# Phi and the memory's term of a pair of heads moved within its slots, and two low parts moved from GpSimd to VectorE

## The chip, the cores and the metric

The kernel runs on one core of a Trainium2 chip. The core has five engines, each with a queue of its own that it works off in order: TensorE (PE, matrix products), VectorE (DVE), ScalarE (ACT), GpSimd (POOL) and SyncE (SP), which here issues every DMA. The metric is the time of one execution on the device in microseconds (us), taken as the median of several runs.

## The reference, cut to what matters

```python
scores = scale * np.matmul(q, k.transpose(0, 1, 3, 2))     # B=2, H=8, S=576, D=64
scores = np.where(causal, -1000000000.0, scores)
a = np.exp(scores - scores.max(-1, keepdims=True)); a /= a.sum(-1, keepdims=True) + 1e-09
local = np.matmul(a, v)
phi = lambda x: np.where(x > 0, x, np.exp(x) - 1.0) + 1.0
q_p = phi(q)
mem_out = (q_p @ M_prev) / (q_p @ z_prev + 1e-06)          # the memory's term
x = sigmoid(beta) * mem_out + (1 - sigmoid(beta)) * local   # -> (1152, 512)
y = ((x @ w1) * (x @ w2)) @ w3 @ w_out                      # 512 -> 1024 -> 1024 -> 512
out = sum over 4 experts of p_e * (relu(y @ e_w1[e]) @ e_w2[e])
```

## The kernel before

**Precision.** Most products are made of two parts of each operand: a high part in a rounded format (a copy or cast) and a low part, which is the difference of the number and its high part. Each product is three passes (`PASSES`): high by low, low by high, high by high. So each operand costs one cast and one subtraction; `lo_pool` makes the subtraction on GpSimd (line 79), `lo_dve` on VectorE (line 82).

**Attention.** The 16 heads are worked on as 8 pairs; pair p has head 2p on partitions 0 to 63 and head 2p + 1 on partitions 64 to 127. `load_pair` loads q and k of a pair (tiles `qd`, `kd`, two buffers each), `stage_h` makes their high and low parts (`qs`, `ks`, one buffer each), `stage_a` the scores (`sc`, line 214) with mask, minimum (DVE, line 220) and exponential (ACT, line 227), `stage_b` the transposes of the probabilities (`pt`, line 254, copied to `pT` by ACT), their product with v (`a`, line 267), the memory's term (`mem`: `b`, line 291, scaled on DVE by `rm` into `xm`), the joining (`join`: `ra` and `xq` on DVE, then `xq + xm` on GpSimd, line 299) and the transposes of the result (`fin`: `x`, line 310, then `xT`). `stage_phi` makes phi of q: an exponential on ACT (`ex`, line 182), a minimum and a maximum with a sum on DVE (lines 185 and 186).

**Slots.** `run_slot(n, ...)` writes the steps of several pairs into one list, each with a number between 0 and 1, and emits them in the order of these numbers: the high and low parts of pair n + 2, phi and scores of pair n + 1, and `stage_b` of pair n, with the fill steps of the weight branch spread between them. `MEM_AT` is the number of the memory's term, `PHI_AT` those of phi. A scheduler then orders the instructions of each engine by its own model of their durations; the order of the program is its priority, not its result.

**The weight branch.** In slots -1 to 0 the eight row tiles of `w_out` are loaded, brought from 64-bit to fp32 by `from64` (two ACT and two DVE instructions, lines 101 to 105, the tile `tu` having one buffer and `tf` three) and split (`wo`). In slots 0 to 3 the product of w3 and w_out is made, one accumulation after another (`wacc0`, `wacc1`, ... line 377; 24 products of 128x512 each, 12 from each of two tiles `w3s`). A `w3s` tile is made by `from64` and then by GpSimd (high part line 76, low part line 79); there are two buffers of it. There is one PSUM buffer for `wacc`, so the first product of `wacc1` waits until ACT and DVE have taken the high and low parts of `wacc0` out (`W0`, lines 382 and 383). In slots 4 to 7 the products with w1 and w2 (`ab`, line 442) and with W (`c`, line 505) take the place of `wacc`; then the second batch's, then the experts (`d` line 613, `o` line 630).

**PSUM for attention.** Scores, `a`, `b` and `x` share two buffers (tag "S").

Of the kernel before, what the change touches and what calls it, by code (L numbers as in the profile page):

```python
# [16 lines left out]


H_AT = (0.5, 0.6, 0.52, 0.62)
PHI_AT = (0.6, 0.7)  # L20
A_AT = (0.2, 0.27, 0.34, 0.41)
T_AT = (0.01, 0.05, 0.09, 0.13, 0.17, 0.21, 0.25, 0.29)
MEM_AT, PV_AT, JOIN_AT, FIN_AT = 0.11, (0.4, 0.48), 0.54, 0.68

WO_SLOTS = (-0.9, -0.8, -0.7, -0.6, -0.3, -0.1, 0.1, 0.2)
W_SLOTS, B_SLOTS, C_SLOTS = (0.0, 4.0), (4.0, 6.4), (6.4, 8.0)
# [7 lines left out]
def kernel(  # L34
# [18 lines left out]
    B, H, D, S = qT.shape  # L53
# [18 lines left out]
    def r32(ap):  # L72
        return ap.bitcast(F32)
# [4 lines left out]
    def lo_pool(dst, src, hi):  # L78
        nc.gpsimd.tensor_sub(dst, src, r32(hi))  # L79

    def lo_dve(dst, src, hi):
        nc.vector.tensor_sub(dst, src, r32(hi))  # L82
# [46 lines left out]
    raw_t, qk_t, phi_t, prob_t = {}, {}, {}, {}  # L129
# [24 lines left out]
    def stage_h(p):  # L154

        if p >= B * H // 2:
            return []
        qd, kd = raw_t[p]
        qk_t[p] = [A1.tile([P, 2, S], F32R, tag=f"{x}s", name=f"{x}s{p}") for x in "qk"]
        qs, ks = qk_t[p]  # L160
        return [
            *zip(
                H_AT,
                (
                    lambda: nc.scalar.copy(qs[:, 0, :], qd),
                    lambda: nc.scalar.copy(ks[:, 0, :], kd),
                    lambda: lo_pool(qs[:, 1, :], qd, qs[:, 0, :]),
                    lambda: lo_pool(ks[:, 1, :], kd, ks[:, 0, :]),
                ),
            )  # L170
        ]

    def stage_phi(p):

        if p >= B * H // 2:
            return []
        qd = raw_t.pop(p)[0]
        ex = A1.tile([P, S], F32, tag="ex", name=f"ex{p}")
        phi_t[p] = phi = A2.tile([P, S], F32, tag="phi", name=f"phi{p}")

        def f0():
            nc.scalar.activation(ex, qd, AF.Exp)

        def f1():
            nc.vector.tensor_scalar(out=ex, in0=ex, scalar1=1.0, scalar2=None, op0=ALU.min)  # L185
            nc.vector.scalar_tensor_tensor(out=phi, in0=qd, scalar=0.0, in1=ex, op0=ALU.max, op1=ALU.add)

        return [*zip(PHI_AT, (f0, f1))]

# [48 lines left out]
    def stage_b(p):  # L238


        b, h = divmod(2 * p, H)
        phi = phi_t[p]
        pt, st = {}, {}
        xq = A2.tile([RP, NQ, 2, D], F32, tag="xq", name=f"xq{p}")

        def trans(x, g):
            def f():
                Pt = prob_t[2 * p + x]
                mine = blocks[g * NB : (g + 1) * NB]
                ps = psT.tile([P, 512], F32, tag="T", name=f"pt{g}_{2 * p + x}")[0:RP, 0 : RP * len(mine)]  # L250
                t = A2.tile([RP, RP * len(mine)], F32, tag=f"pt{g}", name=f"pT{g}_{2 * p + x}")
                for y, (i, j) in enumerate(mine):
                    sl = slice(y * RP, (y + 1) * RP)
                    nc.tensor.transpose(ps[:, sl], Pt[i][:, q0[j] : q0[j] + RP], identF[0:RP, 0:RP])  # L254
                    pt[x, i, j] = t[:, sl]
                nc.scalar.copy(t, ps)
            return f

        def pv(x):
            def f():  # L260
                vn = v4[(2 * p + x) % 4]
                if x == 0:
                    ps = psS.tile([P, 2, 512], F32, tag="S", name=f"a{p}")[0:RP, :, 0 : NQ * (D + 1)]
                    st["a"] = ps.rearrange("p x (i d) -> p x i d", d=D + 1)
                for i in range(NQ):
                    for j in range(i + 1):
                        nc.tensor.matmul(  # L267
                            st["a"][:, x, i, :], lhsT=pt[x, i, j][0 : rows[j]], rhs=vn[0 : rows[j], j, :],
                            start=(j == 0), stop=(j == i),
                        )  # L270
            return f

        def scaled(dst, ps, eps, gate, nm):

            r = A2.tile([RP, 2, NQ], F32, tag=f"r{nm}", name=f"r{nm}{p}")
            for x in range(2):
                nc.vector.tensor_scalar(
                    out=r[:, x, :], in0=ps[:, x, :, D], scalar1=eps, scalar2=gate[0:RP, h + x : h + x + 1],
                    op0=ALU.add, op1=ALU.mult,
                )  # L280
            nc.vector.reciprocal(r, r)
            for x in range(2):
                nc.vector.tensor_mul(dst(x), ps[:, x, :, 0:D], r[:, x, :].unsqueeze(2).to_broadcast([RP, NQ, D]))

        def mem():
            ps = psS.tile([P, 2, 512], F32, tag="S", name=f"b{p}")[0:RP, :, 0 : NQ * (D + 1)]
            m = ps.rearrange("p x (i d) -> p x i d", d=D + 1)
            for i in range(NQ):
                for x in range(2):
                    o = slice(x * D, (x + 1) * D)  # L290
                    nc.tensor.matmul(  # L291
                        m[:, x, i, :], lhsT=phi[o, q0[i] : q0[i] + RP], rhs=mz[o, p, :], start=True, stop=True
                    )
            st["m"] = A2.tile([RP, NQ, 2, D], F32, tag="xm", name=f"xm{p}", bufs=1)
            scaled(lambda x: st["m"][:, :, x, :], m, 1e-6, gm, "m")

        def join():
            scaled(lambda x: xq[:, :, x, :], st["a"], 1e-9, gl, "a")
            nc.gpsimd.tensor_add(xq, xq, st["m"])

        def fin():
            if b:
                xT[b, h // 2] = main.tile([P, 2, S], F32R, tag=f"g{p}", name=f"xT{b}_{h // 2}")
            xt = xT[b, h // 2]

            o0 = 512 - q0[NQ - 1]
            ps = psS.tile([P, 1024], F32, tag="S", name=f"x{p}")[:, o0 : o0 + S]
            for c in range(NQ):
                w = rows[c]
                nc.tensor.transpose(  # L310
                    ps[:, q0[c] : q0[c] + w], xq[0:w, c].rearrange("p h d -> p (h d)"), identF[0:w, 0:w]
                )
            nc.scalar.copy(xt[:, 0, :], ps)
            lo_dve(xt[:, 1, :], ps, xt[:, 0, :])

        return [
            *zip(T_AT, (trans(x, g) for x in range(2) for g in range(4))),
            (MEM_AT, mem), (PV_AT[0], pv(0)), (PV_AT[1], pv(1)), (JOIN_AT, join), (FIN_AT, fin),
        ]

    def run_slot(n, fill):
        steps = stage_h(n + 2) + stage_phi(n + 1) + stage_a(n + 1)
        steps += stage_b(n) if n >= 0 else []
        steps += [((i + 0.5) / len(fill), f) for i, f in enumerate(fill)]
        for _, f in sorted(steps, key=lambda t: t[0]):
            f()
# [152 lines left out]
    for _, f in stage_h(0):  # L479
        f()  # L480
# [57 lines left out]
    for n in range(-1, B * H // 2):  # L538
        if n + 2 < B * H // 2:
            load_pair(n + 2)  # L540
        if n + 1 < B * H // 2:
            load_head(2 * n + 2), load_head(2 * n + 3)
        run_slot(n, sum([f for at, f in fills if n <= at < n + 1], []))
# [59 lines left out]
    for e in range(E):  # L603
        nxt = None
        for c, (c0, cw) in enumerate(CHUNKS):
            hs = []
            for m in range(KF):
                ps = ps3.tile([P, 512], F32, tag="P", name=f"d{e}_{c}_{m}")[:, 0:cw]
                n = 0
# [15 lines left out]
            for tt in range(cw // P):  # L625
                po = ps3.tile([P, 512], F32, tag="P", name=f"o{e}_{c}_{tt}")
                n = 0
# [59 lines left out]
```

## Time and profile before

| | us |
|---|---|
| median of 3 runs | 762.63 (762.61 to 763.99) |
| the profiled execution | 763.01 |
| its span, first to last instruction | 761.2 |
| TensorE busy | 742.5 (98%) |
| VectorE busy | 283.9 (37%) |
| ScalarE busy | 234.7 (31%) |
| GpSimd busy | 224.9 (30%) |

The profiled execution has 1.8 us around its span. TensorE carries the kernel: the chain that ended last lies 95% on it. What it does not spend busy lies nearly all at the start (the first 60 us) and at the end, after the last product.

### The profile page before, as it was taken

The numbers are of one execution on the slowest core, as the hardware profiler recorded it, in microseconds if no ns is written. First come the engines' busy times: TensorE is split into PE (matmuls) and PEld (weight loads), VectorE is DVE, ScalarE is ACT, GpSimd is POOL, SyncE is SP. The second block draws the span as 40 slices with busy tenths as digits, with TensorE's granted clock in tenths as the row PEclk, the third lists the DMA queues.
The fourth block names the chain that finished last, engine by engine and source line by source line (L and its number), as shares of the span: only waits on it lengthen the run. The fifth ranks groups of instructions, "written<-read, shape, count | busy, mean of one in ns | idle before, by whom it ended". The sixth has DMA issues, their size and how long they took to land.

```text
span 761.2 us, 11248 instructions
## 1 busy us (share of the span) xinstructions
PE 742.5 (98%) x4568; PEld 656.5 (86%) x4568; DVE 283.9 (37%) x626; ACT 234.7 (31%) x471; POOL 224.9 (30%) x228
## 2 busy tenths in 40 slices
PE   3899999999999999999999999999999999999997
PEld 2778888899999999999889888898988999888986
DVE  6977557567644135333212112121221112111221
ACT  7976557565644323322202011010111011010110
POOL 2164543444540036004920087000590004300000
PEclk9999999999999999999999999999999999999999
DMA  9873313444510014201410033000241001101010
GB/s 268 282 217 115 104 48 122 134 141 126 174 52 28 2 56 152 58 27 44 126 55 0 1 97 125 0 1 1 57 126 39 1 1 42 28 1 56 0 42 28
DMA packets 48755, 56.69 MB, mean 74 GB/s; under 512 B 15808, under 2 KB 32192, under 8 KB 48704
## 3 DMA queue, kind: packets, MB, share of 16 engines
q1 hardware_dynamic: 48704, 55.97, 24.4%
q8 instruction: 36, 0.59, 0.3%
q14 instruction: 15, 0.12, 0.1%
HBM read 49.41 MB, written 6.55 MB: 74 GB/s over the span
## 4 chain that ended last, share of the span: by engine, by line
PE 95%; DVE 2%; ACT 1%; issue 1%; DMA 0%; SPq 0%; DVEq 0%; ACTq 0%
PE d L613 26%; PE o L630 26%; PE ab L442 14%; PE a L267 7%; PE c L505 7%; PE wacc L377 6%; PE sc L214 4%; PE pt L254 4%; PE b L291 1%; PE x L310 1%; DMA qd<-in_qT_dram 0%; DVE tf_wo L104 0%; DVE tf_wo L105 0%; DVE wo L82 0%; DVE ex L185 0%
## 5 line engine op out<-in xcount | busy, mean ns | idle before, releaser
L630 PE MATMUL o<-el,he 128*128 128x512 f32 x864 | 201.3, 393 | 0.0
L630 PEld LDWEIGHTS o<-el,he 128*128 128x128 f32 x864 | 161.8, 188 | 36.6
L619 ACT ACTIVATE he<-d 128x512 fp32r<-128x512 f32 (+2 forms) x96 | 47.2, 491 | 342.4 <-PE d L613 342.4
L76 POOL TENSOR_SCALAR el<-rel 128x512 fp32r<-128x512 f32 x64 | 40.1, 632 | 258.6 <-PE d L613 188.3
L613 PE MATMUL d<-x2b,el 128*128 128x384 f32 (+1 forms) x768 | 113.7, 308 | 0.0
L613 PEld LDWEIGHTS d<-x2b,el 128*128 128x128 f32 x768 | 113.1, 189 | 0.7
L442 PE MATMUL ab<-xT,ws 128*128 128x288 f32 x768 | 113.1, 298 | 0.0
L620 DVE SCALAR_TENSOR_TENSOR he<-d,he 128x512 fp32r<-128x512 f32 (+2 forms) x96 | 53.5, 558 | 147.7 <-ACT he L619 147.7
L442 PEld LDWEIGHTS ab<-xT,ws 128*128 128x128 f32 x768 | 104.0, 188 | 1.8 <-issue 0.4
L613 PE MATMUL d<-x2a,el 128*128 128x512 f32 x384 | 89.6, 394 | 0.0
L613 PEld LDWEIGHTS d<-x2a,el 128*128 128x128 f32 x384 | 72.0, 188 | 16.8
L79 POOL TENSOR_TENSOR el<-rel,el 128x512 fp32r<-128x512 f32 x64 | 83.4, 1317 | 1.8
L639 DVE SCALAR_TENSOR_TENSOR acc<-o,pr,acc 128x512 f32<-128x512 f32 x27 | 20.3, 751 | 125.7 <-PE o L630 125.7
L505 PE MATMUL c<-hT,W 128*128 128x288 f32 x384 | 58.2, 298 | 0.3 <-DVE x2b L82 0.3
L267 PEld LDWEIGHTS a<-v,pT 114*120 114x120 f32 (+1 forms) x480 | 55.1, 193 | 2.6 <-issue 1.9
L267 PE MATMUL a<-v,pT 114*120 114x65 f32 (+1 forms) x480 | 56.2, 276 | 0.0
L505 PEld LDWEIGHTS c<-hT,W 128*128 128x128 f32 x384 | 52.6, 188 | 0.9 <-DVE x2b L82 0.5
L377 PE MATMUL wacc<-wo,w3s 128*128 128x512 f32 x192 | 50.7, 413 | 0.0
L214 PE MATMUL sc<-ks,qs 64*120 64x120 f32 (+5 forms) x288 | 38.1, 377 | 12.0 <-POOL ks L79 9.4
L227 ACT ACTIVATE P<-P,mn 120x120 f32<-120x120 f32 (+3 forms) x80 | 42.6, 581 | 6.1 <-DVE mn L220 5.9
L377 PEld LDWEIGHTS wacc<-wo,w3s 128*128 128x128 f32 x192 | 36.4, 196 | 8.1 <-issue 0.9
L214 PEld LDWEIGHTS sc<-ks,qs 64*120 64x120 f32 x288 | 25.1, 211 | 21.0 <-POOL ks L79 9.8
(76 smaller groups left out, 598.0 us busy)
## 6 DMA issues: line engine op xcount, KB each, us to landing
rel<-in_moe_w_dram SPq DMA_DIRECT2D x64, 256.0 KB, 2.7
wr<-in_moe_w_dram SPq DMA_DIRECT2D x16, 512.0 KB, 4.1
w3r<-in_moe_w3T_dram SPq DMA_DIRECT2D x16, 512.0 KB, 4.0
wor<-in_moe_w_out_dram SPq DMA_DIRECT2D x8, 512.0 KB, 7.2
wf<-tf SPq DMA_DIRECT2D x16, 256.0 KB, 2.2
wr<-wf SPq DMA_DIRECT2D x16, 256.0 KB, 3.1
v<-in_v_dram SPq DMA_DIRECT2D x16, 150.0 KB, 3.8
qd<-in_qT_dram SPq DMA_DIRECT2D x8, 288.0 KB, 3.5
```

Of the source, the lines that this page charges most:

```text
L76: nc.gpsimd.tensor_scalar(out=dst, in0=src, scalar1=1.0, scalar2=1.0, op0=ALU.mult, op1=ALU.mult)
L79: nc.gpsimd.tensor_sub(dst, src, r32(hi))
L214: nc.tensor.matmul(ps[x][:, c : c + k1 - k0], lhsT=qs[o, a, q0[i] : q0[i] + RP], rhs=ks[o, b, k0:k1], start=(m == 0), stop=(m == 2),)
L227: nc.scalar.activation(Pt[i], Pt[i], AF.Exp, bias=mn[:, i : i + 1], scale=-1.0)
L267: nc.tensor.matmul(st["a"][:, x, i, :], lhsT=pt[x, i, j][0 : rows[j]], rhs=vn[0 : rows[j], j, :], start=(j == 0), stop=(j == i),)
L377: nc.tensor.matmul(wacc[t], lhsT=w3s[u][:, a, c, :], rhs=wo[4 * g + c][:, bb, :], start=(g == 0 and c == 0 and x == 0), stop=(g == 1 and c ...
L442: nc.tensor.matmul(ps[:, 0:HS], lhsT=self.ws[u][:, wi, kk, :], rhs=xT[b, kk][:, xi, a * HS : (a + 1) * HS], start=(n == 0), stop=(n == 3 * ...
L505: nc.tensor.matmul(st["ps"][:, 0:HS], lhsT=Wt[kk][:, wi, d * P : (d + 1) * P], rhs=hT[kk][:, xi, a * HS : (a + 1) * HS], start=(kk == 0 an ...
L613: nc.tensor.matmul(ps, lhsT=ew1[m // 4 * 4 + kk][:, wi, m % 4 * P : (m % 4 + 1) * P], rhs=rhs[:, xi, :], start=(n == 0), stop=(n == 3 * KD ...
L619: nc.scalar.activation(ht[:, 0, :], ps, AF.Relu)
L620: nc.vector.scalar_tensor_tensor(out=ht[:, 1, :], in0=ps, scalar=0.0, in1=r32(ht[:, 0, :]), op0=ALU.max, op1=ALU.subtract,)
L630: nc.tensor.matmul(po, lhsT=hs[kk][:, xi, tt * P : (tt + 1) * P], rhs=ew2[kk][:, wi, :], start=(n == 0), stop=(n == 3 * KF - 1),)
```

## The change

Three things are altered.

1. phi of pair n is made in slot n (numbers 0.22 and 0.3) and not in slot n - 1 (0.6 and 0.7).
2. The memory's term of pair n has the number 0.45 in place of 0.11, which is behind all scores of pair n + 1 in the same slot.
3. The low parts of q and k of the first pair are made on VectorE in place of GpSimd.

```diff
-PHI_AT = (0.6, 0.7)
+PHI_AT = (0.22, 0.3)
-MEM_AT, PV_AT, JOIN_AT, FIN_AT = 0.11, (0.4, 0.48), 0.54, 0.68
+MEM_AT, PV_AT, JOIN_AT, FIN_AT = 0.45, (0.4, 0.48), 0.54, 0.68
...
         qs, ks = qk_t[p]
+        lo = lo_pool if p else lo_dve
...
-                    lambda: lo_pool(qs[:, 1, :], qd, qs[:, 0, :]),
-                    lambda: lo_pool(ks[:, 1, :], kd, ks[:, 0, :]),
+                    lambda: lo(qs[:, 1, :], qd, qs[:, 0, :]),
+                    lambda: lo(ks[:, 1, :], kd, ks[:, 0, :]),
...
     def stage_phi(p):
-        if p >= B * H // 2:
-            return []
...
-        phi = phi_t[p]
+        phi = phi_t.pop(p)
...
-        steps = stage_h(n + 2) + stage_phi(n + 1) + stage_a(n + 1)
-        steps += stage_b(n) if n >= 0 else []
+        steps = stage_h(n + 2) + stage_a(n + 1)
+        steps += stage_phi(n) + stage_b(n) if n >= 0 else []
```

The scheduler makes a new order of the whole attention part from it. In the rows below a name's first number is its place in the program (`w3s2` is the third w3 tile, `qs2` belongs to the third pair, `W0` to the first accumulation) and the number behind the underscore that of its buffer. Three places of slot 0 are shown, each before and after.

GpSimd, from the first w3 tile on, before:

```order
L76 TENSOR_SCALAR w3s0_371<-tf_l30_365 128x512
L79 TENSOR_TENSOR w3s0_371<-tf_l30_365,w3s0_371 128x512
L76 TENSOR_SCALAR w3s1_380<-tf_l31_374 128x512
L79 TENSOR_TENSOR w3s1_380<-tf_l31_374,w3s1_380 128x512
L76 TENSOR_SCALAR w3s2_489<-tf_l32_483 128x512
L79 TENSOR_TENSOR w3s2_489<-tf_l32_483,w3s2_489 128x512
L79 TENSOR_TENSOR qs2_305<-qd2_299,qs2_305 128x576
L79 TENSOR_TENSOR ks2_306<-kd2_301,ks2_306 128x576
```

And after:

```order
L76 TENSOR_SCALAR w3s0_366<-tf_l30_360 128x512
L79 TENSOR_TENSOR w3s0_366<-tf_l30_360,w3s0_366 128x512
L76 TENSOR_SCALAR w3s1_375<-tf_l31_369 128x512
L79 TENSOR_TENSOR w3s1_375<-tf_l31_369,w3s1_375 128x512
L79 TENSOR_TENSOR qs2_300<-qd2_294,qs2_300 128x576
L79 TENSOR_TENSOR ks2_301<-kd2_296,ks2_301 128x576
L76 TENSOR_SCALAR w3s2_467<-tf_l32_461 128x512
L79 TENSOR_TENSOR w3s2_467<-tf_l32_461,w3s2_467 128x512
```

The two low parts of the third pair stand ahead of the third w3 tile now, and stood behind it.

VectorE, from the sixth w3 tile's conversion to the low part of `W0`, before:

```order
L104 SCALAR_TENSOR_TENSOR tf_l35_638<-tf_l35_638,tu_l35_639 128x512
L105 SCALAR_TENSOR_TENSOR tf_l35_638<-w3r5_585,tf_l35_638 128x512
L277 TENSOR_SCALAR ra0_578<-a0_514,gl_59 120x5 x2
L281 RECIPROCAL ra0_578<-ra0_578 120x10
L283 TENSOR_TENSOR xq0_321<-a0_514,ra0_578 120x5x64 x2
L82 TENSOR_TENSOR W0_60<-wacc0_409,W0_60 128x512
```

And after:

```order
L104 SCALAR_TENSOR_TENSOR tf_l35_633<-tf_l35_633,tu_l35_634 128x512
L105 SCALAR_TENSOR_TENSOR tf_l35_633<-w3r5_583,tf_l35_633 128x512
L276 TENSOR_SCALAR rm0_539<-b0_527,gm_58 120x5 x2
L185 SCALAR_TENSOR_TENSOR phi2_971<-qd2_294,ex2_970 128x576
L280 RECIPROCAL rm0_539<-rm0_539 120x10
L282 TENSOR_TENSOR xm0_538<-b0_527,rm0_539 120x5x64 x2
L184 TENSOR_SCALAR ex3_1278<-ex3_1278 128x576
L276 TENSOR_SCALAR ra0_576<-a0_494,gl_59 120x5 x2
L280 RECIPROCAL ra0_576<-ra0_576 120x10
L282 TENSOR_TENSOR xq0_316<-a0_494,ra0_576 120x5x64 x2
L82 TENSOR_TENSOR W0_60<-wacc0_386,W0_60 128x512
```

Five steps stand ahead of `ra` and `W0` that were elsewhere: the scaling of the first pair's memory term, the second half of phi of pair 2 and the first half of that of pair 3.

TensorE, from the last products of `wacc0` to the first of `wacc1`, before:

```order
L377 MATMUL wacc0_409<-wo7_121,w3s1_380 128x512 x3
L254 MATMUL pt0_2_670<-identF_81,P0_2_309 120x120
L254 MATMUL pt0_2_670<-identF_81,P1_2_310 120x120 x2
L254 MATMUL pt0_2_670<-identF_81,P2_2_311 120x120
L254 MATMUL pt1_2_679<-identF_81,P2_2_311 120x120 x2
L254 MATMUL pt1_2_679<-identF_81,P3_2_312 120x120 x2
L254 MATMUL pt2_2_690<-identF_81,P3_2_312 120x120 x2
L254 MATMUL pt2_2_690<-identF_81,P4_2_313 120x120 x2
L254 MATMUL pt3_2_718<-identF_81,P4_2_313 120x120 x3
L377 MATMUL wacc1_587<-wo0_114,w3s2_489 128x512 x3
```

And after, from the memory's term of the first pair on:

```order
L290 MATMUL b0_527<-mz_99,phi0_315 120x65 x10
L266 MATMUL a0_494<-v1_101,pT0_1_391 120x65 x3
L266 MATMUL a0_494<-v1_101,pT1_1_422 120x65 x4
L266 MATMUL a0_494<-v1_101,pT2_1_433 120x65 x4
L266 MATMUL a0_494<-v1_101,pT3_1_471 120x65 x3
L376 MATMUL wacc0_386<-wo7_121,w3s1_375 128x512 x3
L253 MATMUL pt0_2_665<-identF_81,P0_2_302 120x120
L253 MATMUL pt0_2_665<-identF_81,P1_2_303 120x120 x2
L253 MATMUL pt0_2_665<-identF_81,P2_2_304 120x120
L253 MATMUL pt1_2_674<-identF_81,P2_2_304 120x120 x2
L253 MATMUL pt1_2_674<-identF_81,P3_2_305 120x120 x2
L376 MATMUL wacc1_585<-wo0_114,w3s2_467 128x512 x3
```

Fifteen transposes stood between the two accumulations, and eight do now; the memory's term of the first pair, which stood among the transposes before the second pair's scores, is now inside the second half of `a`.

## Rows read from the trace of the kernel before

**Rows 1.** Page, part 1: busy us (share of span) and instructions of TensorE.

```profile
PE 742.5 (98%) x4568; PEld 656.5 (86%) x4568; DVE 283.9 (37%) x626; ACT 234.7 (31%) x471; POOL 224.9 (30%) x228
```

**Rows 2.** Busy us by stretch: PE, PEld, DVE, ACT, POOL; then granted clock, DMA share, GB/s.

```profile
0.00:20.00 20.00, 8.40 (x48) 5.92 (x50) 14.01 (x37) 14.51 (x27) 4.58 (x14) 1.00 0.94 266
...
60.00:80.00 20.00, 20.00 (x165) 16.83 (x164) 15.89 (x42) 15.15 (x28) 8.33 (x9) 1.00 0.44 132
```

**Rows 3.** Timeline of the start: start us, us, engine, line, operation [idle before].

```profile
4.86 0.67 ACT L165 CAST qs<-qd 128x576 fp32r<-128x576 f32 x1 [0.68 <-DMA qd<-in_qT_dram]
5.62 1.40 POOL L79 TENSOR_TENSOR qs<-qd,qs 128x576 fp32r<-128x576 f32 x1 [3.45 <-DMA kd<-in_kT_dram]
...
6.02 0.66 ACT L166 CAST ks<-kd 128x576 fp32r<-128x576 f32 x1
...
6.97 1.62 POOL L79 TENSOR_TENSOR ks<-kd,ks 128x576 fp32r<-128x576 f32 x1
7.37 1.84 DVE L186 SCALAR_TENSOR_TENSOR phi<-qd,ex 128x576 f32<-128x576 f32 x1
...
8.64 2.88 PE L214 MATMUL sc<-ks,qs 64*120 64x120 f32 x24 [8.64 <-POOL ks L79]
```

**Rows 4.** Timeline of VectorE: phi's two steps and a low part, GpSimd idle.

```profile
14.68 0.45 DVE L185 TENSOR_SCALAR ex<-ex 128x576 f32<-128x576 f32 x1
...
16.82 0.76 DVE L186 SCALAR_TENSOR_TENSOR phi<-qd,ex 128x576 f32<-128x576 f32 x1
...
64.00 0.75 DVE L82 TENSOR_TENSOR xT<-x,xT 128x576 fp32r<-128x576 f32 x1
```

**Rows 5.** Timeline: the memory's term of two pairs, and ScalarE's wait for a load.

```profile
19.35 1.87 PE L291 MATMUL b<-mz,phi 64*120 64x65 f32 x16
...
26.43 0.68 ACT L101 ACTIVATE tu_wo<-wor 128x512 uint32<-128x512 uint16 x1 [0.23 <-DMA wor<-in_moe_w_out_dram]
...
87.09 1.27 PE L291 MATMUL b<-mz,phi 64*120 64x65 f32 x20
```

**Rows 6.** Timeline of TensorE from the end of wacc0 to wacc1.

```profile
52.54 0.96 PE L377 MATMUL wacc<-wo,w3s 128*128 128x512 f32 x3
53.35 0.98 PE L254 MATMUL pt<-identF,P 120*120 120x120 f32 x8
54.65 0.99 PE L254 MATMUL pt<-identF,P 120*120 120x120 f32 x7 [0.32 <-ACT pT L256]
55.41 5.72 PE L377 MATMUL wacc<-wo,w3s 128*128 128x512 f32 x24
```

**Rows 7.** Timeline of GpSimd: the third w3 tile, then the third pair's q.

```profile
47.02 0.81 POOL L76 TENSOR_SCALAR w3s<-tf_l 128x512 fp32r<-128x512 f32 x1 [2.49 <-PE wacc L377]
47.91 1.30 POOL L79 TENSOR_TENSOR w3s<-tf_l,w3s 128x512 fp32r<-128x512 f32 x1
49.17 1.42 POOL L79 TENSOR_TENSOR qs<-qd,qs 128x576 fp32r<-128x576 f32 x1
```

**Rows 8.** Timeline of ScalarE at that place.

```profile
47.62 0.68 ACT L165 CAST qs<-qd 128x576 fp32r<-128x576 f32 x1 [0.30 <-PE sc L214]
...
50.12 0.67 ACT L102 ACTIVATE tf_l<-w3r 128x512 f32<-128x512 f32 x1
```

**Rows 9.** Timeline of VectorE up to the low part of W0.

```profile
50.83 1.68 DVE L104 SCALAR_TENSOR_TENSOR tf_l<-tf_l,tu_l 128x512 uint32<-128x512 uint32 x1 [1.77 <-ACT tf_l L102]
52.54 0.69 DVE L105 SCALAR_TENSOR_TENSOR tf_l<-w3r,tf_l 128x512 uint32<-128x512 uint32 x1
53.15 0.35 DVE L277 TENSOR_SCALAR ra<-a,gl 120x5 f32<-120x5 f32 x2
...
54.59 0.68 DVE L82 TENSOR_TENSOR W<-wacc,W 128x512 fp32r<-128x512 f32 x1
```

**Rows 10.** Timeline of TensorE: the first products of wacc0.

```profile
42.32 4.84 PE L377 MATMUL wacc<-wo,w3s 128*128 128x512 f32 x12
```

**Rows 11.** A stretch of these products, columns as in rows 2.

```profile
44.00:46.00 2.00, 2.00 (x6) 1.52 (x6) 1.85 (x3) 1.26 (x2) 0.54 (x1) 1.00 0.69 194
```

## The prediction

> **What bounds the kernel now.** I read the shares of the engines first, then busy time by stretch, then the waits, and last the timelines of single engines in the first 60 us. TensorE is busy for 742.5 of 761.2 us [rows 1]. The stretches show where the rest lies: of the first 20 us TensorE has 8.4 busy, and from 60 us on a stretch of 20 us is full [rows 2]. So from there no wait of another engine counts, and the change can act only on what TensorE does in the first 60 us, or by making a wait where there is none. The first product starts at 8.64, released by the low part of the first pair's k on GpSimd [rows 3]. The next thing to see is the step from the first w3 accumulation to the second: 3 products from 52.54, 15 transposes, and `wacc1` from 55.41 on [rows 6]. There is one buffer for these sums, and the low part of `W0` that frees it starts on VectorE at 54.59 and lasts 0.68, so it ends at 55.27 [rows 9]. The 15 transposes cover this with 0.14 us to spare. That is the tightest place after the start, and the order shows that the change takes its cover away.
>
> **The start (third part of the change).** GpSimd takes 1.40 and 1.62 for the two low parts [rows 3]; VectorE takes 0.75 for one of that size [rows 4]. On VectorE the first can start when the cast of q ends (5.53), the minimum of `ex` (0.45) stands between, and the second needs the cast of k (6.68) [rows 3, 4]. It ends at about 7.5 in place of 8.59: TensorE starts 1.1 us earlier. VectorE pays two times 0.75 and gets back that phi no longer runs beside GpSimd, 1.84 against 0.76 [rows 3, 4]. This gain does not reach the end. At 26.43 ScalarE waits for a slice of `w_out` [rows 5]; the queue of loads has the same order up to there, so that slice lands when it did, and with the new order the exponentials of the second pair and two copies of transposes are queued behind that instruction. I follow the copies: TensorE needs the third `pT` of the first head copied before it can go on with the second head's transposes, and eight instructions of ScalarE stand between that and the one that waited at 26.43. Followed on from there by the durations of the same instructions before, I get both kernels level at about 42 us, with the first pair's memory term still to do in the changed one. Bounds: 0 to 1.1 us gained; I take 0.
>
> **The memory's term (second part).** In the kernel before it ran in TensorE's idle time: 16 of its products from 19.35, at a point where the second pair's q and k were not ready [rows 5]. Now the first pair's stands inside the second half of `a`, where TensorE is full. That costs 20 products, 1.27 us [rows 5]. The wait below swallows it, since TensorE has to wait there anyway; it counts only if that wait is absent. In the later slots the term is moved from one full place to another, and the number of stretches of one kind on TensorE stays about the same (274 before, 269 now): 0, with a bound of 0.5 us to either side.
>
> **Phi (first part).** The scheduler hoists phi: phi's minimum of the first three pairs still stands among the first 40 instructions of VectorE. What the new numbers change is where the rest lands, and that is ahead of `W0`. The load of a q tile now waits for phi's second step; behind it on SyncE's queue stand loads of k, v and w3 tiles. q is loaded a slot or more before its scores, so I take 0 for this.
>
> **The new wait at wacc1.** Here the sum is made. (a) GpSimd made the third w3 tile at 47.02 and 47.91 and then q's low part from 49.17 [rows 7]; the order is now q, k, third tile. The cast of the third pair's q starts at 47.62 and lasts 0.68 [rows 8]. I take it there again: it stands at the end of the same series of conversions of w3 tiles, whose links between ScalarE, VectorE and GpSimd are unchanged. So q's low part runs from 48.3 to 49.7, k's to 51.1 (1.42 each), the tile's high part to 51.9 (0.81), its low part to 53.2 (1.30). Before, it ended at 49.2. (b) ScalarE's next `tf` needs that tile's buffer. It started at 50.12 [rows 8], it now starts at 53.2, +3.1, and ends at 53.9. (c) VectorE waits for it: line 104 took 1.68 beside GpSimd's k, and has no GpSimd beside it now, so I take the 0.69 of line 105 for both [rows 9]: the pair ends at 55.3 in place of 53.2. (d) Ahead of `ra` there are now `rm`, its reciprocal and `xm`, which are the twins of `ra`, its reciprocal and `xq` (53.15 to 54.59, 1.44 us [rows 9]), a phi step of 0.76 and a minimum of 0.45 [rows 4]: 2.65 us. `ra` starts at 57.9, the low part of `W0` at 59.4 and ends at 60.1. (e) `wacc1` starts at 60.2 and not at 55.41, 4.8 us later, and seven transposes (55.41 less 54.65, 0.76 us [rows 6]) are still owed. That is 5.5 us. (f) Two things make it less: the cast of q waited 0.30 for TensorE [rows 8], which has done those scores earlier now, and instructions of VectorE follow each other about 0.08 closer than they last (52.54 to 53.15 is 0.61 for a duration of 0.69 [rows 9]), over about six steps 0.5. **Sum: +4.7 us.** TensorE comes to that place at about 55 and waits for about 4 us; behind it in its queue is everything. Bounds: +3.2 if the 1.1 us of the start and GpSimd's shorter times get through, +6 if VectorE's steps run into GpSimd's next high part.
>
> Against the profiled execution (763.01, of which 1.8 lies around the span) this gives 767.7. The median of the runs shown is 762.63, 0.4 below; from it 767.3. I forecast 767.5. A measurement of this kernel can tell about 0.2% (1.5 us) from no change.
>
> **The rivals.** *The gap costs the clock.* Of the first products of `wacc0`, 12 take 4.84 us [rows 10], while the 24 of `wacc1` take 5.72 [rows 6]: 0.40 against 0.24 each, which are the two levels of 1.2 and 2.4 GHz, although the granted clock is shown as 1.00 in that stretch too [rows 11]. TensorE had only scores, transposes and short products before, and the durations fell behind these twelve. If the 4 us of idle time at `wacc1` set the clock back, the next twelve products last 4.84 instead of 2.9, and the time is 2 us more: 769.5. For it: the gap would be the longest since the start. Against it: no gap after the rise is in the trace. The Trainium skill (TensorE: Matmul & The Clock Gate, Part 1: The HAM clock gate) says that idle time throttles the clock and sustained work releases it; by that rule the time would be this 769.5, and no row here shows a fall.
>
> *No wait at wacc1.* The place is the same, the point is when the third w3 tile's low part ends on GpSimd. If it ends by 50 in place of 53, because ScalarE's series of conversions runs three us ahead (its wait at 26.43 gone, the early scores passed on), `W0` is out at about 56.5 and TensorE hardly waits. Then the memory's term is paid, 1.27, less the wait of 0.32 in the transposes [rows 5, 6]: 763.6, no change that can be told. Against it: ScalarE's and VectorE's series also needs TensorE to release the first w3 tile, which was at 47.02 [rows 7].
>
> *The start gets through.* As the second, and the 1.1 us of the start as well as another microsecond of the 11.6 that TensorE is idle in the first 20 [rows 2] are kept: about 761. It needs both, and the load that ScalarE waits for speaks against it [rows 5].
>
> *Phi is not moved at all* (the scheduler hoists it): this is nearly so, and alone would change nothing; the memory's term and the places above are moved all the same.
>
> **How the numbers follow.** Forecast 0.53 (765.5 to 768.5, slower). Clock set back 0.20 (769.5, slower). No wait or a wait under a microsecond 0.19 (763.6; nearly all within 0.2%, 0.03 of it slower). Faster 0.08. So slower 0.76, same 0.16, faster 0.08. The range for 8 in 10 runs from 763.4, which takes in most of the case without a wait, to 770.0, above the case of the clock.
>
> **What would show it.** In the changed kernel's trace: the first scores at about 7.5; `b` of the first pair behind the first 20 products of `wacc0`; an idle gap of 3 to 5 us on TensorE ahead of `wacc1`, put down to VectorE's line 82 (the low part of `W0`); GpSimd with the third w3 tile's low part ending at about 53; no waits of TensorE above a microsecond after 62 us. The durations of the products behind the gap (0.24 or 0.40) decide on the clock. The forecast is wrong if `W0` is out before the eight transposes are done, or if TensorE waits in later slots too, for `xq` or for the w3 tile that GpSimd makes behind the joining.

## The result

| | us |
|---|---|
| before, median of 8 runs beside it | 762.76 (762.42 to 765.95) |
| changed, median of 8 runs | 767.25 (766.90 to 768.24) |
| ratio changed / before | 1.0057, 95% interval 1.0048 to 1.0066 |
| span of the profiled execution, before / changed | 761.2 / 765.2 |

The changed kernel is 4.5 us slower. The forecast was 767.5 with a chance of 0.76 for slower; size and sign came out, but not by the sum that I wrote: three of its terms were off, and the errors nearly cancel.

### The profile after

First the page's line of engine shares for the changed kernel, which answers to [rows 1], and busy time by stretch, columns as in [rows 2]:

```profile
PE 740.3 (97%) x4568; PEld 655.6 (86%) x4568; DVE 288.7 (38%) x628; ACT 235.4 (31%) x471; POOL 223.1 (29%) x226
```

```profile
0.00:20.00 20.00, 8.62 (x46) 5.96 (x46) 14.11 (x40) 15.89 (x30) 1.60 (x12) 1.00 0.92 271
60.00:80.00 20.00, 20.00 (x134) 16.23 (x133) 10.32 (x30) 12.43 (x24) 6.13 (x7) 0.94 0.33 105
```

TensorE is busy for 2.2 us less than before and the span is 4.0 us longer, so it waits 6.2 us more. And from 60 to 80 us, where the first kernel's granted clock was 1.00, it is 0.94.

The waits of TensorE, longest first (who waits, for whom: us in total, times, longest):

```profile
PE sc L213 <- DVE ks L82: 7.6, 1, 7.6
PE wacc L376 <- DVE W L82: 4.1, 1, 4.1
PE sc L213 <- POOL ks L79: 3.0, 1, 3.0
PE pt L253 <- ACT P L226: 2.4, 2, 1.8
```

The first is the start, 1.0 us shorter than the 8.64 of [rows 3]. The second is the new wait at `wacc1`. The third is the stretch that the first pair's memory term has left. TensorE's timeline at the place of [rows 6]:

```profile
52.21 0.95 PE L376 MATMUL wacc<-wo,w3s 128*128 128x512 f32 x3
53.00 0.98 PE L253 MATMUL pt<-identF,P 120*120 120x120 f32 x8
58.07 4.81 PE L376 MATMUL wacc<-wo,w3s 128*128 128x512 f32 x13 [4.09 <-DVE W L82]
```

And the three engines ahead of it, GpSimd [rows 7], ScalarE [rows 8] and VectorE [rows 9], in this order:

```profile
46.47 1.45 POOL L79 TENSOR_TENSOR qs<-qd,qs 128x576 fp32r<-128x576 f32 x1 [3.46 <-ACT qs L166]
47.86 1.42 POOL L79 TENSOR_TENSOR ks<-kd,ks 128x576 fp32r<-128x576 f32 x1
49.23 0.63 POOL L76 TENSOR_SCALAR w3s<-tf_l 128x512 fp32r<-128x512 f32 x1
49.94 1.27 POOL L79 TENSOR_TENSOR w3s<-tf_l,w3s 128x512 fp32r<-128x512 f32 x1
```

```profile
45.72 0.67 ACT L166 CAST qs<-qd 128x576 fp32r<-128x576 f32 x1
...
51.24 0.67 ACT L102 ACTIVATE tf_l<-w3r 128x512 f32<-128x512 f32 x1 [2.93 <-POOL w3s L79]
```

```profile
51.95 0.69 DVE L104 SCALAR_TENSOR_TENSOR tf_l<-tf_l,tu_l 128x512 uint32<-128x512 uint32 x1 [4.76 <-ACT tf_l L102]
...
55.80 0.35 DVE L276 TENSOR_SCALAR ra<-a,gl 120x5 f32<-120x5 f32 x2
...
57.24 0.68 DVE L82 TENSOR_TENSOR W<-wacc,W 128x512 fp32r<-128x512 f32 x1
```

This is the chain of the prediction, link by link: q and k on GpSimd, the third w3 tile behind them, ScalarE's `tf` that waits for the tile, VectorE that waits for `tf` (idle for 4.76 us with `W0` queued behind), and TensorE that waits for `W0`. Only the times are earlier than I had them: the cast of q starts at 45.72, not at 47.62, and `W0` at 57.24, not at 59.4.

TensorE's own windows behind the gap (busy, then granted clock, DMA share, GB/s):

```profile
56.00:58.00 2.00, 0.00 (x0) 1.00 0.89 268
58.00:60.00 2.00, 1.93 (x6) 0.71 0.14 29
60.00:62.00 2.00, 2.00 (x6) 0.50 0.00 0
62.00:64.00 2.00, 2.00 (x16) 0.94 0.15 38
```

The clock was granted in full up to the gap and falls to 0.50, the level of 1.2 GHz, just behind it. The 13 products take 4.64 us from the first to the next instruction (58.07 to 62.71), against 13 x 0.232 = 3.0 at full clock (the 24 of [rows 6] took 5.57 to the next instruction): 1.6 us. The rule of the Trainium skill that the prediction cited for this rival (TensorE: Matmul & The Clock Gate, Part 1: The HAM clock gate) is that idle time throttles the clock; this trace agrees, with 0.50 behind 4.09 us without a product. No fall followed the gap of 3.21 us in the run with the memory's term alone, further down.

**The sum as the trace has it.** `wacc1` starts 2.66 us later (58.07 for 55.41) and owes seven transposes (0.76): 3.4. The clock takes 1.6. That is 5.0 at the end of the second accumulation. At the first product of the experts (`d`) it is 4.0 (360.17 against 356.18). So 1.0 us is regained on the way, with TensorE waiting 0.8 us there for new reasons (`x` for `xq` 0.4, `ab` for ScalarE 0.4).

The gain is in the memory's later terms. One of them in the kernel before, in TensorE's timeline, and one in the changed kernel:

```profile
213.99 0.43 PE L291 MATMUL b<-mz,phi 64*120 64x65 f32 x4
214.34 1.85 PE L442 MATMUL ab<-xT,ws 128*128 128x288 f32 x12
216.12 0.64 PE L291 MATMUL b<-mz,phi 64*120 64x65 f32 x8
216.69 1.87 PE L442 MATMUL ab<-xT,ws 128*128 128x288 f32 x12
218.48 0.63 PE L291 MATMUL b<-mz,phi 64*120 64x65 f32 x6
```

```profile
170.46 1.27 PE L290 MATMUL b<-mz,phi 64*120 64x65 f32 x20
171.66 2.00 PE L441 MATMUL ab<-xT,ws 128*128 128x288 f32 x13
```

Before, three of the later terms are split into pieces between the products `ab`, and each piece holds TensorE longer than its share: 4 products 0.35, 8 products 0.57, while 20 in a row hold it 1.20. Start to start, the terms of 141, 175 and 214 us took 1.83, 1.35 and 1.83 us; behind the scores they stand in one row, and 1.4 us are saved over the three.

### The profile page after: what moved, and what is told of

Its sections match the earlier page's. It is cut to its first block, busy times and chain, and to the rows that moved or that the text cites. A ratio compares the mean times of both kernels' runs of the same rounds, so it can differ in the third digit from the quotient of the medians.

```text
span 765.2 us, 11257 instructions
## 1 busy us (share of the span) xinstructions
PE 740.3 (97%) x4568; PEld 655.6 (86%) x4568; DVE 288.7 (38%) x628; ACT 235.4 (31%) x471; POOL 223.1 (29%) x226
## 4 chain that ended last, share of the span: by engine, by line
PE 90%; DVE 3%; ACT 2%; issue 1%; POOL 1%; DMA 1%; SPq 0%; POOLq 0%; DVEq 0%; ACTq 0%
PE d L612 26%; PE o L629 26%; PE ab L441 13%; PE c L504 7%; PE a L266 6%; PE wacc L376 5%; PE sc L213 3%; PE pt L253 3%; PE b L290 1%; DMA wor<-in_moe_w_out_dram 1%; POOL w3s L79 1%; PE x L309 1%; DVE P L219 1%; DVE tf_wo L105 0%; ACT P L226 0%
## 5 line engine op out<-in xcount | busy, mean ns | idle before, releaser
L618 ACT ACTIVATE he<-d 128x512 fp32r<-128x512 f32 (+2 forms) x96 | 47.2, 491 | 342.4 <-PE d L612 342.4
L376 PE MATMUL wacc<-wo,w3s 128*128 128x512 f32 x192 | 53.0, 424 | 4.1 <-DVE W L82 4.1
L213 PE MATMUL sc<-ks,qs 64*120 64x64 f32 (+5 forms) x288 | 37.8, 379 | 12.1 <-DVE ks L82 7.6
```

The lines of the kernel that those rows point to most:

```text
L213: nc.tensor.matmul(ps[x][:, c : c + k1 - k0], lhsT=qs[o, a, q0[i] : q0[i] + RP], rhs=ks[o, b, k0:k1], start=(m == 0), stop=(m == 2),)
L376: nc.tensor.matmul(wacc[t], lhsT=w3s[u][:, a, c, :], rhs=wo[4 * g + c][:, bb, :], start=(g == 0 and c == 0 and x == 0), stop=(g == 1 and c ...
L618: nc.scalar.activation(ht[:, 0, :], ps, AF.Relu)
```

## The experiments

The theory after the result: the loss is the wait at `wacc1`, made by GpSimd's order (q and k of pair 2 ahead of the third w3 tile), and the clock's fall behind it. Rivals: the displaced memory term is the loss, and the wait only shows it; the low parts or phi are; the clock is not part of it.

### The three parts, each alone

Phi alone: the maps in the slot of their own pair, ahead of the memory's term, all else as before.

```diff
-PHI_AT = (0.6, 0.7)
+PHI_AT = (0.02, 0.1)
...
+        steps += stage_phi(n) + stage_b(n) if n >= 0 else []
```

> The kernel before with the maps phi of a pair made in the slot of its own output (places 0.02 and 0.1, so that they stand ahead of the memory's term at 0.11) and nothing else. Theory (phi costs nothing: VectorE has them done before TensorE asks): 762.7 us, within 0.2% of before, the piece at the second block's sum as before. Rival (the late phi delays the memory's products): 763.5 to 765, with waits of TensorE's memory products for VectorE's phi.

Measured: 762.98 us against 762.79 for the kernel before beside it, ratio 1.0002 (0.9993 to 1.0011; all ratios from here on are to the kernel before). Phi moved by itself costs nothing that can be told.

The memory's term alone:

```diff
-MEM_AT, PV_AT, JOIN_AT, FIN_AT = 0.11, (0.4, 0.48), 0.54, 0.68
+MEM_AT, PV_AT, JOIN_AT, FIN_AT = 0.45, (0.4, 0.48), 0.54, 0.68
```

> The kernel before with another part alone: the memory's term behind the scores (its place 0.45 instead of 0.11), low parts on GpSimd and the maps phi as before. Theory (the wait at the second block's sum is the loss, and nothing of it comes from the low parts): TensorE waits there for the copy of the first block's sum as in the changed kernel, 3.5 to 5 us, the granted clock falls to 0.5 behind it, and without the start's gain the time is about 1 us above the changed kernel: 768.2 us, between 767 and 769.5. Rival (the wait needs the low parts too, because they shift the conversions): no wait over 1 us, 763.

Measured: 767.74 us, ratio 1.0059 (1.0047 to 1.0071). TensorE's timeline, then GpSimd's:

```profile
54.43 0.98 PE L254 MATMUL pt<-identF,P 120*120 120x120 f32 x8
58.62 3.23 PE L377 MATMUL wacc<-wo,w3s 128*128 128x512 f32 x13 [3.21 <-DVE W L82]
```

```profile
47.19 1.44 POOL L79 TENSOR_TENSOR qs<-qd,qs 128x576 fp32r<-128x576 f32 x1 [3.45 <-ACT qs L165]
48.59 1.42 POOL L79 TENSOR_TENSOR ks<-kd,ks 128x576 fp32r<-128x576 f32 x1
49.98 0.61 POOL L76 TENSOR_SCALAR w3s<-tf_l 128x512 fp32r<-128x512 f32 x1
```

GpSimd's order is turned, and the wait is there, without the low parts moved; at 3.2 us it is a little below the 3.5 to 5 expected. In the execution with the profile (766.3 us) the 13 products take 3.08 us: there the clock did not fall, against what the theory expected. Of the five executions this one and one more, with mean granted clocks of 1.000 and 0.999, took 766.3 and 766.2; the three at 0.997, 0.988 and 0.996 took 767.7, 767.7 and 769.0; the median is one of these. That the clock fell in those three is not shown: there is no trace of them.

The low parts alone:

```diff
+        lo = lo_pool if p else lo_dve
...
+                    lambda: lo(qs[:, 1, :], qd, qs[:, 0, :]),
+                    lambda: lo(ks[:, 1, :], kd, ks[:, 0, :]),
```

> The kernel before with one part of the change alone: the first pair's low parts of q and k on VectorE. The memory's term stays where it was, so the piece on TensorE after the first w3-block's sum is the 15 transposes and 24 products of before. Theory (the loss is the wait at the second block's sum, which the moved memory's term opens): first scores at 7.6 instead of 8.64, no wait at the second block's sum beyond 0.5 us, the start's gain of about 1 us reaches the end: 761.7 us, between 761.2 and 762.7. Rival (the gain at the start is swallowed at about 42 us, as I put it in the prediction): 762.8, no change. Rival (the low parts on VectorE are what makes the loss): 765 or more.

Measured: 765.51 us, ratio 1.0034 (1.0022 to 1.0045): the theory's number is missed by nearly 4 us, and the second rival's is met. The part that I took for harmless, even a gain, is slower by itself. TensorE and GpSimd show why:

```profile
51.31 0.98 PE L255 MATMUL pt<-identF,P 120*120 120x120 f32 x8
55.78 1.65 PE L255 MATMUL pt<-identF,P 120*120 120x120 f32 x7 [3.48 <-ACT pT L257]
57.10 7.84 PE L378 MATMUL wacc<-wo,w3s 128*128 128x512 f32 x24
```

```profile
46.81 1.43 POOL L79 TENSOR_TENSOR qs<-qd,qs 128x576 fp32r<-128x576 f32 x1 [3.44 <-ACT qs L166]
48.20 1.40 POOL L79 TENSOR_TENSOR ks<-kd,ks 128x576 fp32r<-128x576 f32 x1
49.58 0.61 POOL L76 TENSOR_SCALAR w3s<-tf_l 128x512 fp32r<-128x512 f32 x1
```

GpSimd's order is turned here too. The first transposes come 2.0 us earlier than in [rows 6], but the copies of `pT` stand on ScalarE behind the conversion of the w3 tiles, which waits for the late tile. So the same cause, met by TensorE one step sooner (at the transposes, not at `wacc1`), and with the same fall of the clock (granted 0.50 from 56 to 60 us): the 24 products take 7.68 us to the next instruction, not 5.57. Either part alone makes the scheduler turn the order of GpSimd, so both losses, 4.95 and 2.7 us, hold the same late tile, and the changed kernel's 4.5 is not their sum.

### The cause taken away

The changed kernel with pair 2's low parts on VectorE as well; they fall into the 4.76 us in which it waits:

```diff
-        lo = lo_pool if p else lo_dve
+        lo = lo_pool if p not in (0, 2) else lo_dve
```

> The changed kernel with the low parts of pair 2's q and k on VectorE too, where they fall into its idle time ahead of the third w3 tile; GpSimd then makes that tile's parts 2.8 us earlier. TensorE's order of instructions is that of the changed kernel. Theory (the wait at the second block's sum is GpSimd's q and k ahead of the w3 tile, then VectorE's queue in order, then the copy): the tile's parts end near 48.4 instead of 51.2, the copy of the first sum ends near 55.2 instead of 58.0, the wait falls from 4.1 to about 1.2 us, and the granted clock stays at 1.00 there: 767.3 - 2.8 - 1.6 + up to 1 (what was regained behind the clock's fall) = 763 to 764, at most 764.5. Rival (the loss is the memory's term itself, in every slot, and the wait only shows it): the wait goes but the time stays at 766 or more.

Measured: 762.78 us, ratio to before 0.9999 (0.9990 to 1.0008), 4.5 us below the changed kernel, with TensorE's instructions in the same order. GpSimd, then TensorE:

```profile
44.63 0.85 POOL L76 TENSOR_SCALAR w3s<-tf_l 128x512 fp32r<-128x512 f32 x1 [1.71 <-PE wacc L376]
45.56 1.60 POOL L79 TENSOR_TENSOR w3s<-tf_l,w3s 128x512 fp32r<-128x512 f32 x1
```

```profile
54.73 3.24 PE L376 MATMUL wacc<-wo,w3s 128*128 128x512 f32 x13 [1.39 <-DVE W L82]
```

The third tile is made by 47.2 instead of 51.2, `wacc1` starts 3.3 us earlier, and its 13 products take 3.07 us. Two low parts on another engine give back the whole loss, with 1.39 us of the wait left. This shows the cause. The same edit does it without the memory's term: the kernel with the low parts of pairs 0 and 2 on VectorE, further down, has TensorE's instructions in the order of the low parts alone, and takes 761.90 us where that took 765.51.

### The clock by itself

Fourteen products whose result nobody reads, put into the gap; everything that the changed kernel computes is still computed:

```diff
+            if t == 1:
+                dum = psM.tile([P, 512], F32, tag="M0", name="dum", bufs=1)
+                for y in range(14):
+                    nc.tensor.matmul(dum, lhsT=w3s[u - 1][:, 0, y % 4, :], rhs=wo[y % 8][:, 0, :], start=True, stop=True)
```

> The changed kernel with 14 products of 128x512 added behind the first block's sum, into a PSUM buffer that nobody reads: 14 x 0.232 = 3.2 us of work for TensorE in the gap of 4.1 us. It computes all that the changed kernel computes. Theory (about 1.6 us of the loss are the products behind the gap at the lower clock): the copy of the first sum still ends near 58, the gap is filled, the granted clock stays at 1.00 from 58 to 63 and the time falls although work was added: 765.7, between 765.2 and 766.5; if what the clock took is regained later anyway, 767.3. Rival (the clock is not part of it): 767.3, or up to 770 if the added products delay the transposes behind them and these matter.

Measured: 765.84 us, ratio to before 1.0039 (1.0026 to 1.0052): 1.4 us below the changed kernel with 3.2 us of work added. TensorE's timeline and windows:

```profile
52.00 3.37 PE L377 MATMUL dum<-wo,w3s 128*128 128x512 f32 x14
55.21 0.98 PE L253 MATMUL pt<-identF,P 120*120 120x120 f32 x8
57.69 2.31 PE L380 MATMUL wacc<-wo,w3s 128*128 128x512 f32 x9 [1.49 <-DVE W L82]
```

```profile
58.00:60.00 2.00, 2.00 (x11) 1.61 (x10) 0.00 (x0) 0.00 (x0) 1.92 (x3) 1.00 0.04 8
```

`W0` frees the buffer nearly when it did (57.69 against 58.07), the products behind it take 0.24 each, and the clock stays at 1.00. So the clock's fall is worth about 1.4 of the 4.5 us, by an estimate with two reservations: the buffer came free 0.38 us earlier here, and behind the gap TensorE's order is not that of the changed kernel. The intervals of the two ratios overlap (1.0048 to 1.0052); the products' 0.24 us against up to 0.43 in the changed kernel are the firmer sign.

### Two buffers for the sums

If `wacc1` has another buffer, it need not wait for `W0`:

```diff
-            wacc[t] = psM.tile([P, 512], F32, tag="M1", name=f"wacc{t}", bufs=1)
+            wacc[t] = psM.tile([P, 512], F32, tag=f"M{1 - t % 2}", name=f"wacc{t}", bufs=1)
```

On the changed kernel:

> The changed kernel with the sums of the w3-blocks in two PSUM buffers by turns, so that the second block's sum need not wait until the first is copied out; all else as changed, though the scheduler may set the products of the second sum earlier. Theory (the wait for that copy and the clock's fall behind it are the whole loss): no wait over 1 us between 50 and 62 us, granted clock 1.00 there, start's gain kept: 762 us, between 761.3 and 763.5. Rival (the late VectorE queue is the loss, whatever buffer the sum has: what comes next waits for VectorE as long): 766 to 767.5.

Measured: 769.90 us, ratio 1.0088 (1.0074 to 1.0103). Both numbers are missed; the wait is gone and the kernel is slower still. TensorE now waits one step later, for the joining `xq`, whose row scaling stands on VectorE behind the late tile:

```profile
59.28 0.71 PE L309 MATMUL x<-identF,xq 114*128 114x114 f32 x5 [2.37 <-POOL xq L298]
```

With pair 2's low parts on VectorE:

> The changed kernel with two buffers for the sums (769.9 us) and pair 2's low parts on VectorE. TensorE's order of instructions is that of the changed kernel with two buffers. Theory (the loss there is the late third w3 tile, which holds the row scaling xq and so the first transposes x): the wait for xq falls by 2.4 us or more and the time to 762.5 us or less. Rival (the order that two buffers bring to the changed kernel costs by itself, 3.4 us of waits behind 60 us): 765 to 767.

Measured: 766.84 us, ratio 1.0050 (1.0037 to 1.0063). The wait for `xq` is gone and 3.1 us with it, and the rest is the rival's: with two buffers the scheduler makes another order in the changed kernel, and that costs 4 us against the same kernel with one buffer. In the two profiled executions waits make little of it: TensorE no longer waits for `W0` (1.4 us) and 1.4 us less at three smaller places, but 2.0 us more at the products `ab` and 1.7 more at the transposes `pt`, 0.8 us more in all. The greater part, 2.9 us, is time in which TensorE is busy with the same products; 0.85 of it is that the first accumulation's 20 products took 5.99 us and not 5.14, the rest stays open.

On the kernel before, and with the first pair's low parts on VectorE:

> The kernel before with the sums of the w3-blocks in two PSUM buffers by turns. Theory: TensorE does not wait for a copy there in the kernel before, so a second buffer has nothing to take away: 762.6 us, within 0.3% of before. Rival (the copy holds the order of before too, and a free buffer gains some of it): 761 or less. It is the yardstick for the same edit on the changed kernel.

> The kernel before with the first pair's low parts on VectorE and the sums in two PSUM buffers by turns, the memory's term and phi where they were. Theory: the start's gain of about 1 us, plus what the second buffer gives by itself: 761.5 us, between 760.8 and 762.5. Rival (gain at the start swallowed): 762.7.

Measured: 761.08 us, ratio 0.9970 (0.9959 to 0.9981), and 761.64, ratio 0.9980 (0.9971 to 0.9988). The yardstick is no yardstick: a second buffer gains about 2 us in the kernel before (I had expected nothing), and the early start gains nothing on top of it. No wait went away there: TensorE's waits sum to 14.5 us against 14.6, and it is busy for 741.0 us against 742.5. So the second buffer acts through the order that the scheduler makes with it, with either sign; why one order takes TensorE longer than another was not taken apart.

### What the early start and the early term are worth

The kernel before with the low parts of pairs 0 and 2 on VectorE, memory's term and phi unmoved, with one buffer and with two:

```diff
+        lo = lo_pool if p not in (0, 2) else lo_dve
...
+                    lambda: lo(qs[:, 1, :], qd, qs[:, 0, :]),
+                    lambda: lo(ks[:, 1, :], kd, ks[:, 0, :]),
```

> The kernel before with the low parts of pairs 0 and 2 on VectorE; the memory's term and phi where they were, one buffer for the sums. With pair 0's alone TensorE waited 3.5 us for ScalarE's copies pT, which stood behind the third w3 tile. Theory (the third w3 tile behind GpSimd's q and k of pair 2 is what holds ScalarE and VectorE, whichever of the two TensorE then meets first): the tile's low part ends near 47.5 instead of 51.5, no wait over 1 us at 50 to 60 us, granted clock 1.00, and the start's gain of 1.0 us arrives: 761.6 us, between 760.8 and 762.3. Rival (the start's gain is swallowed elsewhere, the low parts of pair 0 are worth nothing): 762.8. Rival (more low parts on VectorE hold the copy of the sum): 764 or more.

> The same with two buffers for the sums. Two buffers alone gave 761.1 on the kernel before, two buffers with pair 0's low parts 761.6, there with TensorE waiting 0.5 us for GpSimd's second w3 block. Theory (that wait and the late third w3 tile ate the start's gain): 760.2 us, between 759.5 and 760.9. Rival (with two buffers TensorE meets another bound, the w3 tiles' conversion, and the start's gain is swallowed): 761.1 to 761.6.

Measured: 761.90 us, ratio 0.9989 (0.9979 to 0.9999), and 760.92, ratio 0.9968 (0.9956 to 0.9980). TensorE's timeline with one buffer:

```profile
54.79 0.99 PE L255 MATMUL pt<-identF,P 120*120 120x120 f32 x7 [0.32 <-ACT pT L257]
55.54 5.70 PE L378 MATMUL wacc<-wo,w3s 128*128 128x512 f32 x24
```

The wait of 3.48 us is gone, and ScalarE waits 0.71 us for the third w3 tile in place of 2.93. But that tile ends at 50.6 in this execution and not near 47.5 as expected: GpSimd now waits 3.59 us for TensorE's first w3 products, which start at 43.33 here and started at 42.06 with the low parts alone, in the same order.

The early start is worth some 0.7 us between the medians, barely told from nothing. The 12 executions spread from 760.41 to 764.66, and the profiled one (762.76) has nothing of it: TensorE waits 1.84 us for ScalarE's exponentials at 24 us (1.13 with the low parts alone), `wacc1` starts no earlier than the 55.41 of [rows 6], and the experts' first product when it did before (356.21 against 356.18). With two buffers the 760.92 lies between the theory's range and the rival's, and is not told from the 761.08 without the early start.

Last, the changed kernel with pair 2's low parts on VectorE and only the first pair's term back in its old place:

```diff
-        return [*zip(PHI_AT, (f0, f1))]
+        return [*zip(PHI_AT if p else (0.02, 0.1), (f0, f1))]
...
-            (MEM_AT, mem), (PV_AT[0], pv(0)), (PV_AT[1], pv(1)), (JOIN_AT, join), (FIN_AT, fin),
+            (MEM_AT if p else 0.11, mem), (PV_AT[0], pv(0)), (PV_AT[1], pv(1)), (JOIN_AT, join), (FIN_AT, fin),
```

> The changed kernel with pair 2's low parts on VectorE (762.8 us) and with the first pair's memory term and maps phi where they were in the kernel before, so that its 20 products of 1.27 us lie again in the stretch in which TensorE waits for the first scores' softmax; the later pairs keep the changed places. Theory (of the moved memory's term only the first pair's counts, because it leaves a stretch with waits): 762.8 - 1.27 = 761.5 us, between 760.8 and 762.2, and equal to the kernel with pairs 0 and 2 on VectorE and no term moved within 0.6 us. Rival (the first pair's term costs nothing where it is, the later slots' order is what differs): 762.8.

Measured: 760.25 us, ratio 0.9965 (0.9954 to 0.9976), 2.3 us faster than before and 7.0 us faster than the changed kernel: the fastest of all. TensorE waits for neither `W0` nor `xq`:

```profile
18.42 2.26 PE L290 MATMUL b<-mz,phi 64*120 64x65 f32 x18 [1.03 <-DVE mn L219]
...
54.44 0.99 PE L253 MATMUL pt<-identF,P 120*120 120x120 f32 x7 [0.32 <-ACT pT L255]
55.19 5.70 PE L376 MATMUL wacc<-wo,w3s 128*128 128x512 f32 x24
```

Two things can be read from it. Against the kernel with the changed place for all pairs (762.78) it gains 2.5 us, of which the expectation had 1.27: the first pair's term belongs in the stretch with waits, and its old place also brings back the fifteen transposes ahead of `wacc1`, which removes the wait of 1.39. And against the kernel with no term moved (761.90) it gains 1.65 us, which I had expected to be within 0.6 of nothing. The later pairs' terms in one row give 1.4 of it: start to start, all eight terms take 11.23 us in this trace and 12.64 in that one.

## Why the prediction came out, point by point

- **What bounds the kernel.** Right: the change acts in the first 60 us, and the tight place was `wacc1`, whose cover of 0.14 us the order took away.
- **The start.** First scores at 7.61, forecast 7.5. The wrong step is the time at which the series of conversions ends. ScalarE's wait for the slice of `w_out` [rows 5] did not stay at 26.43; that instruction ran at 25.42 without a wait for a load, and the series ran 1.9 us earlier by the cast of q (45.72 for 47.62). I had taken the series' end over from before. It is the step (a) from which the sum started. The early start is not all of it: that cast starts at 46.45 with the memory's term alone and at 46.08 with the low parts alone. That the gain of the start by itself "does not reach the end" is not refuted: with the late tile taken away it was worth some 0.7 us with one buffer, barely told from nothing, and nothing that could be told with two.
- **The memory's term.** "The wait below swallows it" holds for the first pair's as long as the wait is there; without the wait it counts, and together with the cover that it displaces it is worth 2.5 us. For the later slots I put 0 with a bound of 0.5. The term was mis-sized: they give 1.4 to 1.65 us back, because they are no longer split into pieces. I had counted stretches of one kind over the whole kernel (274 and 269) and not looked at what was in them.
- **Phi.** 0, as forecast, and by a run of its own. But its new numbers are not what puts its two steps ahead of `W0`: with the memory's term moved alone they stand there too (54.28 and 55.99 us on VectorE).
- **The wait at wacc1.** The mechanism (a) to (e) is shown in all links, and by the experiment that takes q and k off GpSimd. This term was mis-sized: it measured 3.4 us with the transposes owed and not 5.5 less 0.8, nearly the bound of 3.2 that I gave for a start that gets through.
- **The clock.** Given as a rival with 0.20, on top of the full wait; it came in addition to the shorter one, 1.6 us in the trace and 1.4 between the runs. The argument against it ("no gap after the rise is in the trace") was no argument: that a trace does not show a state speaks neither way.
- **The sum.** Forecast +4.7 for the wait. Trace: 3.4 (wait) + 1.6 (clock) - 1.4 (later terms) + 0.8 (new waits), with - 0.4 not assigned, is 4.0 on the span; 4.5 between the medians. The forecast was right by the mechanism; that its size came out to 0.3 us is luck, for the errors cancel.
- **What I did not see.** That the low parts alone turn GpSimd's order. I had put the whole loss on the order of the three parts together and held the third for a gain that is lost on the way.

## What to carry over

When an edit moves where work is done, read the queue of the engine that it is taken from, too: taking two instructions off GpSimd at 6 us turned its order at 47 us, and that cost more than they had. A wait on an engine with a queue in order was removed here by what stands at its head, not by a buffer at its end: in the changed kernel the second buffer only moved the wait to `xq`, while two instructions on an idle engine took 2.7 of its 4.1 us away, and the clock's fall with them. And of a term that is moved, ask for each of its places whether it lay in a wait (move it and you pay for it) or was split into pieces by its neighbours (move it and you gain).

## What the runs showed of the hardware

- A gap of 4.09 us on TensorE in the middle of the kernel was followed by 1.2 GHz (granted clock 0.50 from 60 to 62 us, 13 products in 4.64 us), and so was one of 3.48 with the low parts alone (24 products in 7.68 us); one of 3.21 us with the memory's term alone was not (13 products in 3.08 us). Fourteen idle products in the first of these gaps were cheaper than the gap by 1.4 us between the medians.
- In these traces the granted clock that is shown for the first 45 us does not tell how fast the products run. The two profiled executions below have the same order on TensorE up to 52 us; from 34 to 36 us one shows 1.00, the other 0.50, and the same 24 products `a` take 4.92 us in both, 0.20 each, where 28 of them later take 3.15, 0.11 each (pair 2 on VectorE with one buffer and with two; window, then timeline):

```profile
34.00:36.00 2.00, 2.00 (x12) 1.00 0.46 153
...
31.82 4.92 PE L266 MATMUL a<-v,pT 114*120 114x65 f32 x24
```

```profile
34.00:36.00 2.00, 2.00 (x12) 0.50 0.57 166
...
31.85 4.92 PE L266 MATMUL a<-v,pT 114*120 114x65 f32 x24
```

- The moment at which the products become fast differs between executions: the first accumulation's 20 products, at the same place, took 5.31 us with pair 2 on VectorE and 6.61 us in the changed kernel, with 1.00 shown in both.
- A piece of a few small products between others holds TensorE about 0.1 us or more beyond its share (of the memory's products 4 took 0.35 us and 8 took 0.57, where 20 in a row took 1.20).
